# A spectral gated mix on one core: half of the filter loads issued from GpSimd, most exchanges from SyncE, the job list written anew

## The chip, the cores and the metric

The kernel runs on one core of one Trainium2 chip. The metric is the device time of one execution in microseconds. Before the change the median of three runs is 132.87 us (132.73 to 132.93). One more execution was taken with the hardware profiler: 132.51 us, with a span of 130.7 us from its first to its last instruction.

## The reference

```
x = A_x                                   # 1 x 2048 x 1024, bf16
g = sigmoid((x * gate_w).sum(-1, keepdims=True))
a = irfft2(rfft2(x) * (A_w_r + 1j * A_w_i))    # filters 2048 x 513
b = irfft2(rfft2(x) * (B_w_r + 1j * B_w_i))
out = g * a + (1 - g) * b
```

One real image of 2048 rows and 1024 columns is taken to its two-dimensional spectrum, multiplied by two complex filters, taken back twice, and the two results are mixed row by row with a gate. `B_x` is not used.

## The kernel before

The transforms are matrix products on TensorE. The 2048 rows are split as 32 x 64, the columns are folded into four classes of 256. All the work is cut into *jobs*, and one table, `ORDER`, lists the jobs in one order for the whole kernel. A job's name is followed by its arguments; the last letter is the engine or queue that does it (a ScalarE, d VectorE, p GpSimd, s SyncE). `Prog.add` (L202) puts each operation on its engine's list in the order of the table and finds from the keys that it reads and writes which earlier operations it needs; `emit` (L246) then writes each engine's list with waits. So each engine works strictly in its order, and an operation that waits holds up all behind it on that engine, DMA issues included. PSUM is handed out in four units of two banks: a matmul job takes the unit that was given back longest ago (`take`, `give`, L341 to L348), which also follows the table.

The jobs, in the order of the computation:

- `load.x.g.half` brings in one half of group g of x (256 KB, eight groups). `fold` adds and subtracts mirrored columns on VectorE for groups 0 to 3 (`FOLDED`); the others (REV) are only copied in reverse. `s1m`/`s1e`: first row transform (32 points) on TensorE and its eviction from PSUM. `egen` makes signed copies of its matrix E, `sig0` is a first small Sigmoid on ScalarE, `warm` and `keep` are matmuls of zeros.
- `s2m`/`s2e`: the column transform; it needs all of stage 1. `s4m`/`s4e`: the 64-point row transform. Both exist for p = 0 to 7 and for h = 1 and h = 0, the upper and the lower half of the 513 column frequencies.
- `swap.p.h` is an exchange: two DMAs within SBUF that put the even partitions' data on the odd ones and the other way round, 128 KB each. `xneg.p.h` flips signs behind it, on VectorE or ScalarE.
- `load.W.h.b.m.f` loads m blocks of filter f (0 A, 1 B) from block b on, for half h: four DMAs each (real and imaginary part, two row directions), pieces of 512 or 514 bytes. `load.R` loads the odd rows of block 0, two DMAs. Blocks 1, 2 and 3 lie in `WR`, block 0 in `FR`; both halves use the same place, so that a block of the lower half (h = 0) is loaded once the products of the upper half have used the block there. `w5` saves one column of a block.
- `prod.t.h.c.d` multiplies row block t of half h by its filters on VectorE: t = 0 to 3 uses block 0, 4 to 7 block 1, 8 to 15 blocks 2 and 3. With c = 2 all of it, with c = 0 and 1 (t >= 10, lower half) one half each.
- `s5m.g`/`s5e.g`: the inverse 64-point transform. Groups 16 to 31 need all products of the upper half; groups 8 to 15 need those products of the lower half with c = 2 and c = 1; groups 0 to 7 need all of the lower half.
- The gate: `rev`, `gwm`, `gwe`, `gsm`, `gse`, `rowsum`, `stm`, `ste`, `stx`, `stp`, `zsm`, `zse`, `zst`, `zld` make it and spread it over the partitions through DRAM (`zst` writes, `zld` reads); `rb` and `al` multiply it into the matrix U5 of the last row transform.
- `s6m`/`s6e`: inverse 32-point transform with the gate in it. `s7m`, `s7c`, `s7p`: inverse column transform, one eviction on ScalarE and two additions from PSUM on VectorE. `fin` joins mirrored columns, `store` writes the output.

Filter loads before all stand on SyncE, but for the R loads on GpSimd; of the sixteen exchanges seven are on SyncE, seven on GpSimd, two on ScalarE. A DMA issue occupies its queue's engine, and it waits in that queue's order: `dma` is L312/L313, `copy` L315 to L319, `mult` L321/L322, `sign` L324 to L328, `minus` L330 to L334, `mm` L336/L337. The order in `ORDER` comes from a search outside the kernel that works with a table of durations; that table is not in the file.

Of the kernel before, what the change touches and what calls it, by code (L numbers as in the profile page):

```python
# [26 lines left out]
load.W.1.2.2.0.s fold.4.0.d fold.0.0.d s1m.7.0 s1m.7.1 s1m.3.1 s1e.1.1.a s1m.4.1 load.CK.s load.W.1.2.2.1.s fold.0.1.d s1e.7.0.a s1m.0.0
s1e.7.1.a s1e.3.1.a s1m.4.0 s1e.4.1.d s1m.0.1 s1m.3.0 load.R.1.0.1.1.s load.W.1.0.1.0.s s1e.0.0.a s1e.4.0.d s1m.1.0 s1e.0.1.a s1e.1.0.a
s1e.3.0.d load.GR.a keep.5.2 s2m.7.1 s2m.5.1 s2e.7.1.d s2e.5.1.d s2m.4.1 s4m.7.1 s4m.5.1 s2m.0.1 s2e.4.1.d rev s4e.7.1.a swap.7.1.a
s4e.5.1.d swap.5.1.a load.W.1.0.1.1.s s2m.6.1 s4m.4.1 s2e.6.1.d s2m.3.1 s4e.4.1.a s4m.6.1 swap.4.1.s s2e.0.1.d s2e.3.1.a s2m.1.1 s4m.3.1  # L30
xneg.7.1.d prod.14.1.2.d gwm s4e.6.1.a xneg.5.1.d load.W.1.1.1.1.s s2e.1.1.a s4e.3.1.a s4m.0.1 load.R.1.0.1.0.p load.W.1.1.1.0.s
prod.15.1.2.d gwe.a s4e.0.1.a prod.10.1.2.d xneg.4.1.d w5.0.a w5.2.a s2m.6.0 prod.11.1.2.d gsm.12.2 s2e.6.0.a swap.6.1.p gsm.8.2 s4m.1.1
prod.9.1.2.d gse.12.2.a s4e.1.1.a xneg.6.1.d load.VC.s s2m.2.1 swap.1.1.s gsm.10.2 gse.8.2.a prod.8.1.2.d prod.13.1.2.d s2e.2.1.a s4m.6.0
gse.10.2.a gsm.4.2 s4e.6.0.a swap.3.1.p prod.12.1.2.d gse.4.2.a keep.1.2 xneg.1.1.d gsm.6.2 xneg.3.1.a s4m.2.1 prod.6.1.2.d swap.0.1.p
gse.6.2.a prod.3.1.2.d gsm.0.2 w5.1.a s4e.2.1.a xneg.0.1.a swap.6.0.s gse.0.2.a w5.3.a s2m.4.0 s2m.0.0 s2m.5.0 s2e.4.0.a s2e.0.0.a gsm.14.2
gse.14.2.a s4m.4.0 prod.2.1.2.d s2e.5.0.a s4e.4.0.a prod.1.1.2.d s4m.0.0 s4m.5.0 gsm.2.2 s4e.0.0.a gse.2.2.a s2m.2.0 s2m.1.0 swap.2.1.s
prod.0.1.2.d xneg.6.0.d rowsum.0.d s4e.5.0.a prod.7.1.2.d load.W.0.2.2.1.s xneg.2.1.d rowsum.1.d s2e.2.0.a load.W.0.2.2.0.s s2e.1.0.a stm
prod.5.1.2.d swap.4.0.p load.W.0.0.1.0.s s2m.7.0 s2m.3.0 ste.a xneg.4.0.d s4m.1.0 load.W.0.0.1.1.s swap.0.0.p load.R.0.0.1.1.p prod.4.1.2.d
s4m.2.0 s2e.7.0.a s4m.7.0 xneg.0.0.d s2e.3.0.a s4e.1.0.a s4e.2.0.a s4e.7.0.a prod.8.0.2.d stx.s s5m.24 prod.12.0.0.d swap.5.0.p s5m.30
load.R.0.0.1.0.p s4m.3.0 s5e.24.a s5e.30.a rowsum.2.p stp.2.d swap.1.0.s keep.8.2 swap.7.0.s s5m.23 prod.13.0.0.d prod.9.0.2.d stp.0.d  # L40
# [222 lines left out]
def bass_gated_mix__spectral_gfnet__spectral_gfnet__prompt_kernel(nc, A_x, A_w_r, A_w_i, B_x, B_w_r, B_w_i, gate_w, out):  # L263
# [44 lines left out]
    P = Prog()  # L308
# [81 lines left out]

    def keep(k, n):
# [444 lines left out]
```

## Time and profile before

| what | value |
|---|---|
| median of 3 runs | 132.87 us (132.73 to 132.93) |
| the profiled execution | 132.51 us, span 130.7 us |
| TensorE busy | 109.0 us, 83% of the span |
| VectorE busy | 105.1 us, 80% |
| ScalarE busy | 92.5 us, 71% |
| GpSimd busy | 48.8 us, 37% |
| moved by DMA | 25.56 MB, mean 196 GB/s |
| mean granted TensorE clock | 0.961 |

Busy time does not count DMA issues on the hardware queues (SPq, ACTq); those of GpSimd are shown on POOL as instructions of their own. A row in order of time gives start, length, engine, line, operation, tiles and count, and in brackets how long the engine was idle before it and what ended that. In rows of groups the figures behind the bar are busy time, mean duration of one in ns, and idle time before the group.

### The profile page before, as it was taken

The page shows a single profiled execution, that of the slowest core. Times are in us where ns is not written, and L with a number is a line of the kernel's source. Part 1 is how long each engine was busy: PE and PEld are TensorE (multiplying, and loading weights), DVE is VectorE, ACT ScalarE, POOL GpSimd, SP SyncE. Part 2 cuts the span into 40 slices and gives each one's busy share as a digit, 9 for nine tenths or more (in the row PEclk, how much of TensorE's full clock was granted, in tenths as well). Part 3 has the DMA queues.
Part 4 walks back from the last instruction along what each step waited for, and adds up shares of the span by engine and source line. Part 5 has one row for each costly group of instructions (what it writes and reads, how often), then busy time and mean ns, then how long its engine had stood idle before and what let it go on. Part 6 is the DMA issues. An engine that isn't in the chain of part 4 may idle for free.

```text
span 130.7 us, 3713 instructions
## 1 busy us (share of the span) xinstructions
PE 109.0 (83%) x1553; PEld 87.0 (67%) x1553; DVE 105.1 (80%) x135; ACT 92.5 (71%) x121; POOL 48.8 (37%) x58
## 2 busy tenths in 40 slices
PE   6964997899999969979987835999999987999900
PEld 3343876668677756927675525999999986798300
DVE  0216858698999699973999799799979999999990
ACT  0750696521999599998999982999388995679110
POOL 3000000012170002950310000999345894999480
PEclk9997799999999999999999996799999999999995
DMA  3899999978689729999756784600000312174347
GB/s 85 284 351 351 365 327 331 294 167 209 214 222 302 245 90 242 276 346 303 230 183 176 203 271 153 291 0 5 5 0 0 115 50 86 75 278 170 115 151 259
DMA packets 27507, 25.56 MB, mean 196 GB/s; under 512 B 2834, under 2 KB 23074, under 8 KB 27234
## 3 DMA queue, kind: packets, MB, share of 16 engines
q1 hardware_dynamic: 22544, 18.41, 47.4%
q10 hardware_dynamic: 3714, 3.95, 8.9%
q0 software_dynamic: 1232, 2.96, 6.3%
q8 instruction: 12, 0.20, 0.7%
q14 instruction: 5, 0.04, 0.1%
HBM read 16.90 MB, written 4.20 MB: 161 GB/s over the span
## 4 chain that ended last, share of the span: by engine, by line
PE 37%; DMA 20%; DVE 14%; ACT 8%; SPq 7%; issue 6%; ACTq 4%; DVEq 1%
PE PS L337 37%; DMA WP<-in_A_x_dram 9%; DVE WP L322 8%; DMA WR<-in_A_w_i_dram 7%; SPq L313 7%; ACTq L313 4%; ACT WP L317 4%; DVE FR L753 4%; DMA WP<-WP 3%; ACT FR L317 2%; DVE WP L472 1%; ACT L667 1%; ACT WP L332 1%; DVEq L775 1%; DVE WR L753 0%
## 5 line engine op out<-in xcount | busy, mean ns | idle before, releaser
L317 ACT ACTIVATE WP<-PS 128x1024 bf16<-128x1024 f32 (+1 forms) x51 | 49.1, 1019 | 15.2 <-PE PS L337 14.9
L317 ACT ACTIVATE FR<-PS 128x1024 bf16<-128x1024 f32 (+1 forms) x44 | 36.2, 890 | 12.3 <-PE PS L337 9.2
L337 PE MATMUL PS<-FR,WP 128*128 128x128 bf16 (+2 forms) x384 | 32.6, 246 | 1.3 <-DVE FR L753 1.0
L337 PEld LDWEIGHTS PS<-FR,WP 128*128 128x128 bf16 x384 | 28.4, 130 | 5.1 <-DVE FR L753 1.4
L337 PE MATMUL PS<-CK,WP 128*128 128x64 bf16 x512 | 20.2, 202 | 5.4 <-DVE WP L322 4.7
L337 PEld LDWEIGHTS PS<-CK,WP 128*128 128x128 bf16 x512 | 19.3, 119 | 8.0 <-DVE WP L322 5.3
L759 POOL TENSOR_TENSOR WR<-FR 128x512 bf16<-128x512 f32 x15 | 20.4, 1369 | 7.5 <-DVE FR L753 7.2
L319 DVE CAST WP<-PS 128x1024 bf16<-128x1024 f32 x14 | 16.5, 1218 | 3.4 <-PE PS L337 3.3
L753 DVE TENSOR_TENSOR FR<-PS,FR 128x512 f32<-128x512 f32 x28 | 17.7, 678 | 1.2 <-ACT FR L317 1.0
L322 DVE TENSOR_TENSOR WP<-FR,WR 128x1024 bf16<-128x1024 bf16 (+1 forms) x18 | 14.6, 866 | 3.1 <-issue 2.2
L337 PE MATMUL PS<-F,FR 128*128 128x128 bf16 x256 | 15.9, 219 | 1.2 <-ACT FR L317 0.6
L337 PEld LDWEIGHTS PS<-F,FR 128*128 128x128 bf16 x256 | 14.7, 98 | 3.1 <-ACT FR L317 1.6
L337 PE MATMUL PS<-WP 128*128 128x256 bf16 (+1 forms) x128 | 13.4, 265 | 3.8 <-DMA WP<-in_A_x_dram 2.7
L337 PEld LDWEIGHTS PS<-WP 128*128 128x128 bf16 x128 | 10.6, 106 | 6.9 <-DMA WP<-in_A_x_dram 3.5
L322 DVE TENSOR_TENSOR WP<-WP,WR 128x2048 bf16<-128x2048 bf16 x12 | 14.3, 1217 | 0.0
L337 PE MATMUL PS<-FR 128*128 128x480 bf16 (+3 forms) x52 | 11.7, 364 | 2.7 <-ACT WP L317 1.4
L322 POOL TENSOR_TENSOR FR<-FR,F 128x1024 bf16<-128x1024 bf16 x3 | 7.3, 2438 | 16.0 <-DMA FR<-c_U 16.0
L759 DVE TENSOR_TENSOR WR<-FR 128x512 bf16<-128x512 f32 x13 | 12.6, 990 | 0.0
L313 POOL DMA_DIRECT2D FR<-FR x8 | 4.5, 565 | 17.9 <-PE PS L337 17.9
L577 POOL COPY FR<-FR 128x128 bf16<-128x128 bf16 x1 | 0.3, 292 | 27.3 <-DMA FR<-c_RG 27.3
L337 PE MATMUL PS<-WP,CK 128*128 128x512 bf16 (+4 forms) x44 | 8.7, 328 | 0.0
L337 PEld LDWEIGHTS PS<-FR 128*128 128x128 bf16 x52 | 4.2, 112 | 6.5 <-issue 1.6
(54 smaller groups left out, 88.3 us busy)
## 6 DMA issues: line engine op xcount, KB each, us to landing
WP<-in_A_x_dram ACTq DMA_DIRECT2D x9, 256.0 KB, 8.6
out_dram<-WR SPq DMA_DIRECT2D x17, 128.0 KB, 2.1
WP<-in_A_x_dram SPq DMA_DIRECT2D x7, 256.0 KB, 7.9
FR<-FR SPq DMA_DIRECT2D x8, 128.0 KB, 2.9
FR<-FR POOLq DMA_DIRECT2D x8, 128.0 KB, 5.2
FR<-c_U SPq DMA_DIRECT2D x1, 1024.0 KB, 7.2
FR<-c_DI SPq DMA_DIRECT2D x1, 1024.0 KB, 4.8
out_dram<-WR ACTq DMA_DIRECT2D x8, 128.0 KB, 2.3
```

What stands on the lines that cost most here:

```text
L313: return P.add(eng, lambda e: e.dma_start(dst, src), dma=name, **kw)
L317: P.add("act", lambda e: e.activation(dst, src, ACT.Copy), **kw)
L319: P.add(eng, lambda e: e.tensor_copy(dst, src), **kw)
L322: P.add(eng, lambda e: e.tensor_tensor(out=dst, in0=s0, in1=s1, op=ALU.mult), **kw)
L332: P.add("act", lambda e: e.activation(dst, src, ACT.Copy, scale=-1.0), **kw)
L337: P.add("pe", lambda e: e.matmul(o, lh, rh, start=first, stop=last), **kw)
L472: P.add(Q[eng], lambda e: e.tensor_tensor(out=fs, in0=xs(0, 1), in1=xs(511, -1), op=ALU.subtract if k else ALU.add), **kw)
L577: P.add("pool", lambda e: e.tensor_copy(sl(FR, GRo + 128, [(1, 128)]), sl(FR, GRo + 127, [(-1, 128)])), r=["GR"], w=["GRr"])
L667: P.add("act", lambda e: e.activation(sl(ZG, 0, [(1, 32)], np_=64), sl(FR, 20480, [(1, 32)], np_=64), ACT.Sigmoid), r=["zero", ("FR", 40), ...
L753: P.add(Q[eng], lambda e: e.tensor_tensor(out=o, in0=ps(u * 1024, [(1, 512)]), in1=eos(i), op=ALU.subtract if s else ALU.add), r=[("EO", i ...
L759: P.add(Q[eng], lambda e: e.tensor_tensor(out=od, in0=pv[0], in1=pv[1], op=ALU.subtract if s else ALU.add), r=[("PQ", i % NPQ, 0), ("PQ", ...
L775: with nc.Block() as block:
```

## The change

`ORDER` is replaced by another list of the same kinds of jobs. What each job computes is unchanged, and so are `FOLDED`, `HALVED` and `MODE`. In words: x comes in as groups 3, 1, 4, 2, 5, 6, 0, 7 instead of 6, 2, 5, 1, 3, 7, 0, 4; the upper half is transformed from p = 0 upwards and multiplied from block 0 on (t = 1, 0, 3, 2, 4, 6, 5, 7 and then 14 to 12), where it was multiplied from blocks 2 and 3 on; seven of the twelve W jobs stand on GpSimd (28 of 48 DMAs) and five on SyncE; of the exchanges nine are on SyncE, six on GpSimd, one on ScalarE. The gate vector's load (`load.GR`) stands on ScalarE right behind x instead of behind stage 1. `egen.1.2` comes ahead of `sig0`. Of `rb` and `al`, two of four `rb` more are on VectorE. `warm` and `sig0` get one more key to wait for, because block 0 is now also written from GpSimd's queue. The new file is one line shorter ahead of the code, so that a line's number there is one less than here.

The start of the table, and the other edits:

```diff
-load.SM.a zero load.E.1.s load.x.6.0.a warm.12x64x1.14x512x1 load.x.6.1.s load.x.2.1.a egen.1.3 egen.1.1 fold.6.0.d load.x.5.1.s
+load.SM.a zero load.E.1.s egen.1.3 load.x.3.0.a load.E.0.s load.x.3.1.a egen.0.1 fold.3.0.d fold.3.1.d load.x.1.0.a egen.1.1 load.x.1.1.a
...
-                    mm(ps(u * 1024, [(1, nn)]), sl(FR, 20480, [(st, 128)]), sl(FR, 20480, [(1, nn)]), True, True, r=["zero", ("FR", 40), ("FR", 41)], w=banks(u))
+                    mm(ps(u * 1024, [(1, nn)]), sl(FR, 20480, [(st, 128)]), sl(FR, 20480, [(1, nn)]), True, True, r=["zero", ("FR", 40), ("FR", 41), ("W", 3, 1)], w=banks(u))
...
-        P.add("act", lambda e: e.activation(sl(ZG, 0, [(1, 32)], np_=64), sl(FR, 20480, [(1, 32)], np_=64), ACT.Sigmoid), r=["zero", ("FR", 40), ("FR", 41)], w=["ZG"])
+        P.add("act", lambda e: e.activation(sl(ZG, 0, [(1, 32)], np_=64), sl(FR, 20480, [(1, 32)], np_=64), ACT.Sigmoid), r=["zero", ("FR", 40), ("FR", 41), ("W", 3, 1)], w=["ZG"])
```

What stands on GpSimd from `rev` on, before (WP<-WP and FR<-FR are exchanges of the upper and the lower half, FR<-in_ are filter rows of block 0):

```order
L577 COPY FR<-FR 128x128 [waits d_GR]
L313 DMA FR<-in_A_w_r_dram 64x257
L313 DMA FR<-in_A_w_i_dram 64x257
L313 DMA WP<-WP 64x1024 [waits s_act]
L313 DMA WP<-WP 64x1024
```

And in the new order (64x4x257 is 256 pieces of 514 bytes; WR<-in_ are blocks 2 and 3 here):

```order
L576 COPY FR<-FR 128x128 [waits d_GR]
L312 DMA FR<-in_A_w_r_dram 64x257
L312 DMA FR<-in_A_w_i_dram 64x257
L312 DMA FR<-in_B_w_r_dram 64x4x257 [waits s_act,s_pe]
L312 DMA FR<-in_B_w_i_dram 64x4x257
L312 DMA FR<-in_B_w_r_dram 64x3x257
L312 DMA FR<-in_B_w_i_dram 64x3x257
L312 DMA FR<-in_A_w_r_dram 64x4x257
L312 DMA FR<-in_A_w_i_dram 64x4x257
L312 DMA FR<-in_A_w_r_dram 64x3x257
L312 DMA FR<-in_A_w_i_dram 64x3x257
L312 DMA WR<-in_A_w_r_dram 64x8x257
```

Eight loads of block 0 and, from the last of these rows on, eight of blocks 2 and 3 with 512 pieces each (`load.W.1.2.2.0` and `.1`) now stand on GpSimd ahead of its first exchange.

On SyncE, behind the loads of x and of the constants, before (from the fourth exchange on):

```order
L313 DMA WP<-WP 64x1024 [waits s_act]
L313 DMA WP<-WP 64x1024
L313 DMA WR<-in_B_w_r_dram 64x8x256 [waits d_W121,s_act,s_dve]
L313 DMA WR<-in_B_w_i_dram 64x8x256
L313 DMA WR<-in_B_w_r_dram 64x8x256
L313 DMA WR<-in_B_w_i_dram 64x8x256
L313 DMA WR<-in_A_w_r_dram 64x8x256 [waits d_W120]
L313 DMA WR<-in_A_w_i_dram 64x8x256
```

And in the new order, at the same place in the computation:

```order
L312 DMA FR<-FR 64x1024 [waits s_pe,s_act]
L312 DMA FR<-FR 64x1024
L312 DMA WR<-in_A_w_r_dram 64x8x256 [waits d_W120,s_dve]
L312 DMA WR<-in_A_w_i_dram 64x8x256
L312 DMA WR<-in_A_w_r_dram 64x8x256
L312 DMA WR<-in_A_w_i_dram 64x8x256
L312 DMA FR<-FR 64x1024 [waits s_pe,s_act]
L312 DMA FR<-FR 64x1024
```

SyncE issues only filter A of the lower half's blocks 2 and 3 (`load.W.0.2.2.0`), and does so behind four exchanges of the lower half; filter B's four loads (`load.W.0.2.2.1`) stand on GpSimd behind `rowsum.2` and `swap.4.0`.

On VectorE, the sign flips (TENSOR_SCALAR) and the first products of the upper half, before (the d_xs semaphores are exchanges, d_W filter loads):

```order
L328 TENSOR_SCALAR WP<-WP,SM 128x1024 [waits s_act,d_xs71]
L322 TENSOR_TENSOR WP<-WP,WR 128x8x64x4 [waits d_W121,d_W120,s_dve]
L328 TENSOR_SCALAR WP<-WP,SM 128x1024 [waits d_xs51]
L322 TENSOR_TENSOR WP<-WP,WR 128x8x64x4
L322 TENSOR_TENSOR WP<-WP,WR 128x8x64x4 [waits s_dve]
```

And in the new order:

```order
L327 TENSOR_SCALAR WP<-WP,SM 128x1024 [waits s_act,d_xs01]
L321 TENSOR_TENSOR WP<-WP,FR 128x8x64x4 [waits d_R100,d_W101,d_R101,d_W100,s_dve]
L321 TENSOR_TENSOR WP<-WP,FR 128x8x64x4
L318 CAST GSB<-PS 128x4 [waits s_pe]
L321 TENSOR_TENSOR WP<-WP,FR 128x8x64x4 [waits d_xs11,s_act]
L321 TENSOR_TENSOR WP<-WP,FR 128x8x64x4
L327 TENSOR_SCALAR WP<-WP,SM 128x1024 [waits d_xs21]
L327 TENSOR_SCALAR WP<-WP,SM 128x1024 [waits d_xs31]
L321 TENSOR_TENSOR WP<-WP,WR 128x8x64x4 [waits d_W111,d_W110,s_dve]
```

The first product now waits for block 0, which GpSimd loads; blocks 2 and 3, also GpSimd's, are wanted by the ninth product.

More of the change, by code (lines that the diff above doesn't have):

```diff
@@ L27 @@
[L27 to L38, printed above, removed]
```

63 lines of the change are left out of this document (37 added, 26 removed).

## Prediction

> **What bounds the kernel now.** I read the chain of waits first, then the stretches of time with each engine's busy time, then the order of time on VectorE (DVE), ScalarE (ACT), GpSimd (POOL) and SyncE (SP). From the chain, in order of time (start, length, what):
>
> ```profile
> 7.28 12.18 DMA WP<-in_A_x_dram
> ...
> 41.77 4.26 DMA WP<-WP
> ...
> 52.31 7.16 DMA WR<-in_A_w_i_dram
> 59.47 2.16 issue
> ...
> 71.23 2.34 DMA WR<-in_A_w_i_dram
> ...
> 79.88 10.38 PE PS L337 x272
> ```
>
> Up to 19.46 us (7.28 + 12.18) the image x is loading. Then one exchange (WP<-WP) and two filter loads (WR<-in_A) stand on the chain, and at 79.88 the products are done and TensorE can transform them. The stretches (start:end, length, then busy us and count of PE, weight load, DVE, ACT, POOL, then clock, DMA share, GB/s):
>
> ```profile
> 33.40:59.10 25.70, 23.45 (x350) 17.40 (x348) 23.02 (x28) 24.09 (x39) 9.13 (x17) 1.00 0.80 242
> 59.10:79.80 20.70, 15.03 (x281) 11.23 (x281) 17.61 (x25) 18.37 (x22) 1.71 (x3) 1.00 0.77 226
> ...
> 91.30:127.50 36.20, 31.44 (x368) 27.31 (x368) 34.68 (x49) 23.77 (x34) 26.04 (x24) 1.00 0.26 95
> ```
>
> From 33.4 to 79.8 DVE (products) and ACT (PSUM evictions) are both close to full: ACT lacks 1.6 us in the first stretch, DVE 2.7; in the second 2.3 and 3.1. So exchanges and filter loads cost only what DVE or ACT waits for them, and what one wins counts only as far as the other follows. After 91.3 DVE sets the pace (34.68 of 36.20). DVE's waits, in brackets:
>
> ```profile
> 33.42 0.48 DVE L328 TENSOR_SCALAR WP<-WP,SM 128x1024 bf16<-128x1024 bf16 x1
> ...
> 46.06 0.49 DVE L328 TENSOR_SCALAR WP<-WP,SM 128x1024 bf16<-128x1024 bf16 x1 [1.46 <-DMA WP<-WP]
> ```
> ```profile
> 57.44 0.49 DVE L328 TENSOR_SCALAR FR<-FR,SM 128x1024 bf16<-128x1024 bf16 x1 [0.97 <-DMA FR<-FR]
> 57.84 1.22 DVE L322 TENSOR_TENSOR WP<-WP,WR 128x2048 bf16<-128x2048 bf16 x1
> ...
> 61.63 1.83 DVE L322 TENSOR_TENSOR WP<-FR,WR 128x2048 bf16<-128x2048 bf16 x2 [2.17 <-issue]
> ...
> 74.59 8.24 DVE L322 TENSOR_TENSOR WP<-FR,WR 128x2048 bf16<-128x2048 bf16 x10 [0.91 <-DVE PST L322]
> ```
>
> The upper half (h=1) is multiplied from 33.42 to 59.06, the lower half to 82.83. Late transfers cost 1.46 + 0.97 in the one, 2.17 + 0.91 in the other ("issue" ends with load.W.0.2.2.0, the chain's 7.16 us row). Why those loads come late stands on SP's queue:
>
> ```profile
> 47.51 0.65 SPq L313 DMA_DIRECT2D WR<-in_B_w_r_dram  x1
> ...
> 52.31 1.15 SPq L313 DMA_DIRECT2D WR<-in_A_w_i_dram  x1
> ...
> 59.79 0.61 SPq L313 DMA_DIRECT2D FR<-in_B_w_i_dram  x1
> ```
>
> From 47.51 to 60.40 SP does nothing but issue sixteen filter loads, one after another, and every exchange given to it waits behind them.
>
> **The change, part by part.** The sum is made against the profiled execution, 132.51 us (span 130.7); the median of the three runs, 132.87, lies 0.36 above, which I add at the end.
>
> *Loading x and stage 1.* The same bytes in another order, so the last piece of x still lands at about 19.5. Group 7 (a REV group) is now folded behind group 0 on DVE, so some 0.5 us more stand between that landing and the first s2 matmul. ACT now meets a Copy before the Sigmoid, so two tables are loaded instead of one:
>
> ```profile
> L667 ACT ACT_TABLE_LOAD x1 | 1.3, 1283 | 3.6 <-issue 3.6
> ```
>
> That is 1.28 us more, near 7 to 11 us, before x gives ACT much to do; counted at 0 while x hides it, 1.3 if it does not.
>
> *The first exchange.* Now it is swap.0.1, behind three evictions on ACT (s2e.0.1, s2e.1.1, s4e.0.1); before, one stood in front of it:
>
> ```profile
> 28.50 1.02 ACT L317 ACTIVATE WP<-PS 128x1024 bf16<-128x1024 f32 x1 [3.81 <-PE PS L337]
> 29.55 2.59 ACTq L313 DMA_DIRECT2D WP<-WP  x4
> ```
>
> ACT starts at about 26.35 (28.50 less the DVE evictions that led it, plus the 0.5) and issues the exchange at about 30, 0.5 later than 29.55; the sign flip then starts at about 34.0 instead of 33.42. Bounds: 0 to 1.5 us late.
>
> *GpSimd's loads, the price the trace lacks.* POOL now waits for the gate vector (issued on ACT right behind x, so about 20 to 21 instead of 28.8), then issues two R loads, eight loads of block 0 (192 or 256 pieces each) and eight of W.1.2.2 (512 pieces), all before its first exchange. The nearest rows are 64 pieces (the x4 rows and the first) and 128 (the last):
>
> ```profile
> L577 POOL COPY FR<-FR 128x128 bf16<-128x128 bf16 x1 | 0.3, 292 | 27.3 <-DMA FR<-c_RG 27.3
> ```
> ```profile
> 29.06 0.69 POOL L313 DMA_DIRECT2D FR<-in_A_w_r_dram  x1
> ...
> 37.18 2.16 POOL L313 DMA_DIRECT2D WP<-WP  x4 [0.66 <-ACT GW L317]
> 51.46 2.34 POOL L313 DMA_DIRECT2D FR<-FR  x4 [12.13 <-PE PS L337]
> ...
> 65.17 0.63 POOL L313 DMA_DIRECT2D zd<-ZG  x1 [1.04 <-ACT ZG L663]
> ```
>
> 64 pieces take 0.54 (2.16 / 4), 128 take 0.63: 1.4 ns for each further piece, so a 512-piece load takes 0.54 + 448 x 0.0014 = 1.17. Bounds: 0.54 (no cost per piece; the first of a row of issues takes 0.69 anyway), and 4.3 (all of 0.54 proportional: 8.4 ns a piece). I take 1.17, since the 128-piece row is nearest. Then POOL has issued the R loads by 22.5, block 0 by 28.6 (8 x 0.76) and W.1.2.2 by 38.0 (8 x 1.17). Landing, by queue and size:
>
> ```profile
> WR<-in_A_w_r_dram SPq DMA_DIRECT2D x2, 257.0 KB, 11.6
> FR<-FR SPq DMA_DIRECT2D x8, 128.0 KB, 2.9
> FR<-FR POOLq DMA_DIRECT2D x8, 128.0 KB, 5.2
> ```
>
> With 3 to 6 us more, block 0 is there at 32 to 34 (needed at 34.4) and W.1.2.2 at 41 to 44 (needed by the ninth product, about 46.8). Both lie beside the stage-2 work; the margins are about 1 and 3 us.
>
> *Upper half on DVE.* Durations:
>
> ```profile
> L322 DVE TENSOR_TENSOR WP<-WP,WR 128x2048 bf16<-128x2048 bf16 x12 | 14.3, 1217 | 0.0
> L322 DVE TENSOR_TENSOR WP<-FR,WR 128x1024 bf16<-128x1024 bf16 x12 | 7.8, 687 | 0.0
> L328 DVE TENSOR_SCALAR WP<-WP,SM 128x1024 bf16<-128x1024 bf16 x9 | 4.2, 481 | 5.3 <-DMA SM<-c_SM 3.6 <-DMA WP<-WP 1.7
> L319 DVE CAST WP<-PS 128x1024 bf16<-128x1024 f32 x14 | 16.5, 1218 | 3.4 <-PE PS L337 3.3
> ```
>
> Back to back these overlap by 0.08: 1.14 a product, 0.61 a half product, 0.40 a flip, 1.14 an eviction. From its first flip the new order holds 16 products (18.2), six flips (2.4), a small cast and a row-sum step (0.8): 21.4. SP now has nothing but exchanges then, so the waits fall from 2.4 to my estimate of 1.5 (xneg.1.1 on ACT and xneg.3.1, whose exchanges go out just ahead of their use; bounds 0.5 to 4). The upper half ends at 34.0 + 21.4 + 1.5 = 56.9, 2.2 earlier than 59.06.
>
> *Lower half on DVE.* Up to where s5 group 8 may start: ten products (11.4), six half products (3.7), five flips (2.0), the second row-sum step, one s5 eviction and a trifle (1.9): 19.0, so 75.9; six more halves (3.7) end at 79.6, against 82.83. Blocks 0 and 1 are freed and reloaded some 12 us before use. W.0.2.2.0 and W.0.2.2.1 are freed last, at 56.9; SP issues its four by 59.5, POOL, behind rowsum.2 and swap.4.0, by about 63.8 (59.1 + 4 x 1.17). They land by 67; the first half product wants them at 68: no wait, where 2.17 + 0.91 stood. Bounds 0 to 3.
>
> *ACT.* Rows:
>
> ```profile
> L317 ACT ACTIVATE WP<-PS 128x1024 bf16<-128x1024 f32 x50 | 48.7, 1030 | 15.2 <-PE PS L337 14.9
> L326 ACT ACTIVATE FR<-FR,SM 128x1024 bf16<-128x1024 bf16 x2 | 2.3, 1156 | 0.0
> ```
> ```profile
> 59.90 1.94 ACT L317 ACTIVATE WP<-PS 128x1024 bf16<-128x1024 f32 x2 [0.34 <-PE PS L337]
> ...
> 71.35 6.49 ACT L317 ACTIVATE WP<-PS 128x1024 bf16<-128x1024 f32 x7
> 80.96 10.35 ACT L317 ACTIVATE WP<-PS 128x1024 bf16<-128x1024 f32 x11 [3.12 <-PE PS L337]
> ```
>
> An eviction costs 0.93 in a row (6.49 / 7), a flip 1.05. ACT starts 2.15 earlier, takes three more upper-half evictions (2.8) and one more flip, and issues one exchange less (1.3): at about 60 it stands where it stood at 59.55. Then come 15 s5 evictions and one s4 (14.8), two flips (2.1) and the gate (0.2), to 77.1, about when group 8 is ready (75.9 + 0.7 of matmul). The 3.12 us wait at 80.96 goes; the rest of s5 is the same row, 10.35, plus 0.9 for the groups that wait for DVE's last halves: 88.3, against 80.96 + 10.35 = 91.31. DVE meanwhile has five evictions (5.7) and the small work of the gate, and is done by about 88 too. **Gain 3.0 us.** U5 and the gate are on time if they come as early as before; they wait for POOL's zst, now behind swap.7.0, so up to 1 us may go here.
>
> *The tail* keeps the 32 PSUM additions and 13 final additions on DVE (34.68 busy of 36.20): 0, give or take 1. Sum: 132.51 - 3.0 = 129.5, on the median's scale 129.9; I say **129.8**, 127.3 to 131.3 by the bounds above except POOL's.
>
> **The rivals.**
>
> *POOL's long loads are dearer (slower).* With p for a 512-piece load, W.1.2.2 has landed at 22.5 + 8 x (0.54 + 0.4 (p - 0.54)) + 8p + 4 = 29.1 + 11.2p. It delays the ninth product from p = 1.58, costs 1.12 us per 0.1 us beyond it, and eats the gain at p = 1.85. At p = 2.0 it is +4.7: 134.5; at 4.3 far more. For it: no row has over 128 pieces. Against: 64 to 128 pieces cost only 0.09. Chance 0.17.
>
> *VectorE holds up GpSimd's issues (slower).* The products fill DVE almost without a break while POOL issues W.0.1.1.1, W.0.1.1.0 and W.0.2.2.1. If each issue waited out a product, the four of W.0.2.2.1 would come 4 x 1.2 = 4.9 later, at 72 instead of 67: 4 us of wait, 133.5 or so. The x4 row at 51.46 speaks against it: POOL issued four exchanges in 2.34 us with DVE multiplying throughout. Chance 0.07. The Trainium skill (SBUF — State Buffer, § SBUF: two separate sides) says that while VectorE runs in a two-port mode GpSimd cannot write the descriptors of its DMAs, and that SP or ACT should issue them instead, which speaks against this change; by that row the trace does not agree.
>
> *ACT is the bound anyway (about the same).* It was short of work by only 1.6 us of 25.70. If the new order makes it wait 2.5 us for the exchanges whose flips it does in its own queue (1.1, 5.1, 5.0, 4.0, 7.0), where the old had two or three, the gain shrinks to 0.5: 132.4, spread 131.4 to 133.3. Chance 0.20.
>
> **How the numbers follow.** The forecast has 0.56. The measurement tells 0.2% (0.27 us). Faster: 0.56 + 0.10 of the ACT rival = 0.66; same: 0.08 of it; slower: 0.02 of it + 0.17 + 0.07 = 0.26. The range reaches from 127.3 up to 134.5, which takes in the ACT and VectorE rivals and the near end of the first.
>
> **What would show it.** Right: POOL issues of 512 pieces near 1.2 us, W.1.2.2 issued by 40; no DVE wait over 1 us between 45 and 57; the last half product before 81; ACT without the 3 us gap; the first PSUM addition of s7 3 us earlier. Wrong: POOL issues over 1.6 us or DVE waiting for W.1.2.2; ACT idle behind its flips; rb waiting for U5; or new waits in the tail.

## The result and the profile after

The changed kernel took 140.1 us (median of 4 runs, 137.81 to 141.3) beside 132.8 for the kernel before. Two of the four (141.3 and 141.01 us) were slow runs with a lower granted TensorE clock (0.922 and 0.945, beside 0.963 and 0.951 in the others), and the ratio, 1.043 with a 95% interval of 1.034 to 1.052, leaves them out, as all ratios below do with such runs. It is slower, and outside the range of the prediction. In the first profile of it stage 1 is late (128 products in 14.0 us instead of 11.9) and all that follows is shifted, so the comparison is made with a second profile of the same kernel (run `e8_same` below: 139.21 us, span 137.3). Both have the same waits. The group of stage 1's products, first profile and second:

```profile
L336 PE MATMUL PS<-WP 128*128 128x256 bf16 (+1 forms) x128 | 14.0, 278 | 3.6 <-DVE WP L471 3.6
```
```profile
L336 PE MATMUL PS<-WP 128*128 128x256 bf16 (+1 forms) x128 | 11.9, 246 | 3.6 <-DVE WP L471 2.4 <-DVE WP L318 1.0 <-DMA WP<-in_A_x_dram 0.2
```

Where the steps of the prediction came out (us; read from the order of time on VectorE, ScalarE and the queues; a transfer lands at its issue plus its time to landing; "last half product" is the end of the lower half's products):

| | before | forecast | after |
|---|---|---|---|
| first exchange, issued to landed | 29.55 to 33.29 | 30 to 34 | 30.26 to 37.12 |
| first sign flip | 33.42 | 34.0 | 37.14 |
| upper half multiplied | 59.06 | 56.9 | 59.01 |
| last half product | 82.83 | 79.6 | 85.05 |
| stage 5 ends | 91.31 | 88.3 | 94.65 |
| first addition of stage 7 | 95.61 | | 98.74 |
| VectorE ends | 127.45 | | 133.01 |
| span | 130.7 | | 137.3 |

The chain of waits of the changed kernel (second profile), the first exchange and the filter load that stand on it:

```profile
30.26 0.53 ACTq L312
30.83 6.29 DMA WP<-WP
37.14 0.50 DVE WP L327
...
65.26 8.54 DMA WR<-in_B_w_i_dram
```

Before, a later exchange stood on the chain with 4.26 us, and two filter loads with 7.16 and 2.34; now the first exchange has 6.29 and one load 8.54. VectorE's order of time, waits in brackets (second profile):

```profile
37.14 0.49 DVE L327 TENSOR_SCALAR WP<-WP,SM 128x1024 bf16<-128x1024 bf16 x1 [4.71 <-DMA WP<-WP]
...
52.24 1.23 DVE L321 TENSOR_TENSOR WP<-WP,WR 128x2048 bf16<-128x2048 bf16 x1 [0.25 <-ACT WP L325]
...
73.92 0.69 DVE L321 TENSOR_TENSOR WP<-FR,WR 128x1024 bf16<-128x1024 bf16 x1 [1.87 <-DMA WR<-in_B_w_i_dram]
```

One wait of 4.71 us ahead of the first flip, then almost none to the end of the upper half: the new order does hold VectorE's work together, as forecast, but starts it 3.1 late. ScalarE, whose flip waits for an exchange too, stands behind it:

```profile
38.92 1.15 ACT L325 ACTIVATE WP<-WP,SM 128x1024 bf16<-128x1024 bf16 x1 [3.21 <-issue]
```

What GpSimd does meanwhile (first and last load of block 0, first and last of the two 1 MB loads of blocks 2 and 3):

```profile
24.76 0.62 POOL L312 DMA_DIRECT2D FR<-in_B_w_r_dram  x1
...
27.86 0.64 POOL L312 DMA_DIRECT2D FR<-in_A_w_i_dram  x1
28.49 0.71 POOL L312 DMA_DIRECT2D WR<-in_A_w_r_dram  x1
...
33.26 0.69 POOL L312 DMA_DIRECT2D WR<-in_B_w_i_dram  x1
```

A 512-piece load costs 0.69, so the 2 MB are all issued by 33.9, four us earlier than forecast, and lie on the DMA engines just when the exchanges are issued. The final additions on VectorE, in the kernel before and in the changed one:

```profile
L759 DVE TENSOR_TENSOR WR<-FR 128x512 bf16<-128x512 f32 x13 | 12.6, 990 | 0.0
```
```profile
L758 DVE TENSOR_TENSOR WR<-FR 128x512 bf16<-128x512 f32 x13 | 15.4, 1214 | 0.0
```

Thirteen in both, but 2.8 us more on the engine that sets the tail. The mean hides two sizes: in the kernel before three of the thirteen took 1.8 to 2.2 us and the others 0.67 to 0.81, in the changed one five took 1.7 to 2.4 and the others 0.68 to 0.87.

### The profile page after: what moved, and what is told of

It reads as the page before. It is cut to its first block, busy times and chain, and to the rows that moved or that the text cites. A ratio compares the mean times of both kernels' runs of the same rounds, so it can differ in the third digit from the quotient of the medians.

```text
span 139.4 us, 3701 instructions
## 1 busy us (share of the span) xinstructions
PE 112.7 (81%) x1553; PEld 89.4 (64%) x1553; DVE 106.9 (77%) x136; ACT 98.1 (70%) x125; POOL 61.1 (44%) x79
## 4 chain that ended last, share of the span: by engine, by line
PE 47%; DVE 17%; ACT 12%; DMA 11%; issue 6%; ACTq 2%; DVEq 1%
PE PS L336 47%; ACT WP L316 9%; DMA WP<-in_A_x_dram 6%; DVE WP L321 5%; DMA WP<-WP 5%; DVE WR L758 5%; DVE FR L752 5%; ACTq L312 2%; ACT FR L316 2%; ACT FR L325 1%; DVEq L774 1%; DVE FR L318 1%; DVE WP L471 1%; DVE WR L752 0%; DVE WP L327 0%
## 5 line engine op out<-in xcount | busy, mean ns | idle before, releaser
L316 ACT ACTIVATE WP<-PS 128x1024 bf16<-128x1024 f32 (+1 forms) x55 | 53.1, 1030 | 12.3 <-PE PS L336 11.9
L336 PEld LDWEIGHTS PS<-CK,WP 128*128 128x128 bf16 x512 | 20.2, 120 | 6.5 <-ACT WP L316 2.3
L336 PE MATMUL PS<-CK,WP 128*128 128x64 bf16 x512 | 21.3, 206 | 3.1 <-ACT WP L316 1.5
L336 PE MATMUL PS<-F,FR 128*128 128x128 bf16 x256 | 16.6, 223 | 5.0 <-DVE GSB L318 3.9
L318 DVE CAST WP<-PS 128x1024 bf16<-128x1024 f32 x10 | 12.1, 1222 | 5.3 <-PE PS L336 5.3
L321 DVE TENSOR_TENSOR WP<-FR,WR 128x1024 bf16<-128x1024 bf16 (+1 forms) x18 | 14.4, 865 | 2.1 <-DMA WR<-in_A_w_i_dram 2.1
L336 PEld LDWEIGHTS PS<-WP 128*128 128x128 bf16 x128 | 11.6, 111 | 6.3 <-DVE WP L471 4.6
L758 DVE TENSOR_TENSOR WR<-FR 128x512 bf16<-128x512 f32 x13 | 15.4, 1212 | 0.0
L336 PE MATMUL PS<-FR 128*128 128x480 bf16 (+3 forms) x52 | 11.9, 375 | 3.1 <-ACT WP L316 1.7
L327 DVE TENSOR_SCALAR WP<-WP,SM 128x1024 bf16<-128x1024 bf16 x9 | 4.2, 483 | 9.1 <-DMA WP<-WP 5.5
L336 PE MATMUL PS<-WP,CK 128*128 128x512 bf16 (+4 forms) x44 | 9.6, 358 | 0.0
L471 DVE TENSOR_TENSOR WP<-WP 128x1024 bf16<-128x1024 bf16 x8 | 5.2, 685 | 5.3 <-DMA WP<-in_A_x_dram 5.3
```

The costliest lines, as they stand in the source:

```text
L316: P.add("act", lambda e: e.activation(dst, src, ACT.Copy), **kw)
L318: P.add(eng, lambda e: e.tensor_copy(dst, src), **kw)
L321: P.add(eng, lambda e: e.tensor_tensor(out=dst, in0=s0, in1=s1, op=ALU.mult), **kw)
L327: P.add(eng, lambda e: e.tensor_scalar(out=dst, in0=src, scalar1=SM[:, col:col + 1], scalar2=None, op0=ALU.mult), **kw)
L336: P.add("pe", lambda e: e.matmul(o, lh, rh, start=first, stop=last), **kw)
L471: P.add(Q[eng], lambda e: e.tensor_tensor(out=fs, in0=xs(0, 1), in1=xs(511, -1), op=ALU.subtract if k else ALU.add), **kw)
```

## The experiments

Theory A: the filters' bytes that are issued ahead of an exchange, from whichever queue, have to cross the DMA engines first; the new order puts a 1 MB load there. Rival B: stage 1 and the tail lose the time. Rival C: GpSimd's queue pushes the exchanges aside. Theory D: the new tail is dearer by itself. Rival E: ScalarE's row sets the half's end whatever VectorE waits for.

### The 2 MB later

```diff
-gse.6.2.d load.W.1.2.2.0.p swap.2.1.s
+gse.6.2.d swap.2.1.s
...
-swap.7.1.p swap.4.1.p
+swap.7.1.p load.W.1.2.2.0.p swap.4.1.p load.W.1.2.2.1.p
```

> The changed kernel, with the two 1 MB filter loads of the upper half's blocks 2 and 3 put later on GpSimd, one behind each of its first two exchanges, so that they are issued after about 37 us instead of 28.4 to 33.8. Theory A (these 2 MB share the DMA engines with the first exchanges): the first exchange, issued near 31.4 us, lands within 4 us instead of 7.1, the first half product starts by 36 instead of 39.0, the idle times of VectorE (5.5), ScalarE (3.4) and TensorE (3.9 us) go, and the time falls by 2 to 6 us to 134 to 138; the 9th product may now wait for the load, which would eat a part. Rival B (the late stage 1, the tail and the slower final additions make up most of the loss): the exchange may land earlier, but the time falls by less than 1.5 us.

Measured: 144.7 us, 1.091 (1.083 to 1.100). VectorE's order of time:

```profile
32.35 0.49 DVE L327 TENSOR_SCALAR WP<-WP,SM 128x1024 bf16<-128x1024 bf16 x1 [0.54 <-DMA WP<-WP]
...
53.37 4.63 DVE L321 TENSOR_TENSOR WP<-WP,WR 128x2048 bf16<-128x2048 bf16 x4 [4.97 <-DMA WR<-in_B_w_i_dram]
```

The mechanism is as A says: the exchange took 2.7 us and the first flip came 4.8 earlier. The time, 12 us above the kernel before, is a miss for A as for B: the loads, issued from 39.6 and 43.4 on, landed at 46.7 and 53.2, and the 9th product, due at 44.4, waited for an exchange (3.54) and then for them.

### All filter loads from SyncE

```diff
-load.VC.s load.W.1.0.1.0.p
+load.VC.s load.W.1.0.1.0.s load.W.1.2.2.0.s load.W.1.2.2.1.s
...
-load.W.0.1.1.1.p
+load.W.0.1.1.1.s
```

and so on for each `load.W` and `load.R` of GpSimd's; the two 1 MB loads are gone from their later places.

> The changed kernel with all its filter loads issued from SyncE's queue again, in the changed kernel's order, the two 1 MB loads still ahead of the first exchanges and issued at about the same time, 28 to 35 us. Theory A (bytes on the engines at the wrong time, whichever queue issues them): the first exchange lands as late as before, after 37.5 us, and the time stays within 2 us of the changed kernel's 140. Rival C (GpSimd's software queue, with its larger packets, takes the engines' time from the exchanges' small packets): the exchange that ScalarE issues lands within 4 us, by 35.5, and the time falls by over 2 us.

Measured: 147.8 us, 1.115 (1.106 to 1.124). The flip:

```profile
35.28 0.49 DVE L327 TENSOR_SCALAR WP<-WP,SM 128x1024 bf16<-128x1024 bf16 x1 [3.29 <-DMA WP<-WP]
```

The exchange took 5.4 us, between the two expectations: it landed at 35.26, before C's 35.5, but took more than C's 4 us, with three of the first 1 MB load's four transfers ahead of its second DMA. The time is a miss for both. SyncE's own exchanges went out only at 35.4, behind the loads, and the second landed at 40.6. So GpSimd's queue is not the only cause, and without it the order is worse.

### The kernel before with one part of the change

```diff
-load.W.1.1.1.1.s
...
-load.R.1.0.1.0.p load.W.1.1.1.0.s
+load.R.1.0.1.0.p load.W.1.1.1.1.p load.W.1.1.1.0.p
```

(The two loads stood ahead of and behind other jobs; only they moved. They are the two of block 1, not of blocks 2 and 3 as the expectation has it.)

> The kernel before, with one part of the change alone: the two 0.5 MB loads of blocks 2 and 3 counted from the low end (issued by SyncE at 34.5 to 39.9 us before) are issued from GpSimd at 30.3 to 35.3 us, beside the first exchange (issued at 29.55, landed 3.7 us later) and the second (30.9, landed 4.5 us later). Theory A: those two exchanges land 1 to 3 us later, and the first half product starts 1 to 3 us after 33.9; the loads themselves land earlier, so the time is 0 to 2 us longer. Rival C gives the same direction but more: over 3 us on the exchanges, as the software packets go first. Rival B: no change in either, within 0.5 us.

Measured: 133.1 us, 1.003 (0.998 to 1.008): no change that can be told. The flip:

```profile
35.65 0.49 DVE L328 TENSOR_SCALAR WP<-WP,SM 128x1024 bf16<-128x1024 bf16 x1 [1.96 <-DMA WP<-WP]
```

The exchange took 5.9 us instead of 3.7 and the next 6.3 instead of 4.5, but the loads, earlier now, spared as much later: the upper half ended at 58.83 (59.06 before). In that order, then, a later first exchange cost nothing in the end: the wait of 1.46 at 46.06 went.

### The 2 MB held until the first exchange has landed

```diff
             kw = dict(w=keys) if what == "W" else dict(w=[("WR16", f)])
+            if (h, b) == (1, 2):
+                kw["r"] = place(2, 0, 1)[2]
```

> The changed kernel, with the two 1 MB filter loads of the upper half's blocks 2 and 3 made to wait on GpSimd until the first exchange has landed (about 32.5 us), between the changed kernel's 27.3 to 33.8 and the 39.6 to 46.2 of the run that put them behind GpSimd's exchanges. Theory A (2 MB have to cross the DMA engines between the first exchange and the 9th product; the start decides who waits): the first product starts near 33, the loads land near 43 to 44.5, the 9th product (due at 44 to 45 then) waits 0 to 1 us, the last upper product ends near 56 instead of 59.1, and the time falls by 2 to 4 us against the changed kernel's 138 to 140. Rival B (what is lost lies in the lower half and the tail, which start by TensorE and ScalarE, not by this): the upper half ends earlier and the time falls by less than 1 us.

Measured: 137.9 us, 1.041 (1.035 to 1.048), 0.8 below the changed kernel of its group.

```profile
33.49 0.49 DVE L327 TENSOR_SCALAR WP<-WP,SM 128x1024 bf16<-128x1024 bf16 x1 [0.55 <-DMA WP<-WP]
40.90 0.49 DVE L327 TENSOR_SCALAR WP<-WP,SM 128x1024 bf16<-128x1024 bf16 x1 [1.25 <-DMA WP<-WP]
44.29 0.49 DVE L327 TENSOR_SCALAR WP<-WP,SM 128x1024 bf16<-128x1024 bf16 x1 [2.91 <-DMA WP<-WP]
```

The first exchange came in 2.7 us; the third and fourth, now behind the loads, took 6.5 and 8.0. Most of the wait moved behind the fourth product, and the upper half ended at 60.20, not near 56: A holds for each exchange, but the gain that was expected of it does not. B's figure (less than 1 us) came, but not its reason, as the upper half ended no earlier.

### One load early from SyncE; then both

```diff
-load.R.1.0.1.1.s
+load.R.1.0.1.1.s load.W.1.2.2.0.s
...
-gse.6.2.d load.W.1.2.2.0.p swap.2.1.s
+gse.6.2.d swap.2.1.s
```

> The changed kernel with one of the two 1 MB loads of blocks 2 and 3 (upper half, first filter) issued from SyncE at 21 us, behind its R load, where SyncE's queue ran dry and the DMA engines were 70% busy, instead of from GpSimd at 27 to 28.5. Theory A (the bytes that are still to come when the first exchanges go out decide): about 0.7 MB more is over by 28 us, the first exchange lands 1.5 to 3 us earlier than 37.1, the time falls by 0.5 to 2 us against 138.7; block 0's filters may land 1 to 3 us later than 30.5, still ahead of the first product. Rival C (it is GpSimd's queue that pushes the exchanges aside): as one of the two still comes from GpSimd, the first exchange gains less than 1 us.

Measured: 138.2 us, 1.041 (1.030 to 1.052). The bytes were over by 36.8 instead of 41.6, the exchange landed at 37.27 all the same. That misses A's 1.5 to 3 us and is what C expected. The run that followed moves `load.W.1.2.2.1` there as well:

> The run with one 1 MB load issued early from SyncE, with the other one behind it on SyncE too, so that GpSimd's queue holds block 0's filters alone and nothing of it is on the way when the first exchange goes out (29.7 us). Rival C (GpSimd's queue pushes the exchanges aside): the exchange lands within 4.5 us, by 34.3, and the time falls by 1.5 to 3 us against 138.2. Theory A (the bytes, whichever queue): the exchange lands with the last of the filters again, at 36 to 37.5, and the time stays within 1 us.

Measured: 137.6 us, 1.030 (1.019 to 1.040). The first flip in these two:

```profile
37.30 0.49 DVE L327 TENSOR_SCALAR WP<-WP,SM 128x1024 bf16<-128x1024 bf16 x1 [5.39 <-DMA WP<-WP]
```
```profile
36.35 0.49 DVE L327 TENSOR_SCALAR WP<-WP,SM 128x1024 bf16<-128x1024 bf16 x1 [4.60 <-DMA WP<-WP]
```

In the second run GpSimd's queue held block 0 alone. The last of that landed at 33.38, yet the exchange took 6.7 us (7.5 with 1 MB of GpSimd's beside it) and landed at 36.33, with SyncE's load: C falls as the main cause. Set side by side, the exchange lands within 0.7 us of the last filter transfer that was issued ahead of its second DMA, or, where that was over before, 2.1 us after that DMA's issue. What is issued behind it (the changed kernel's second 1 MB, landed at 41.62) does not hold it:

| run | first exchange issued | transfers ahead of it all landed by | it landed | took |
|---|---|---|---|---|
| 2 MB later | 29.64 | 30.52 | 32.32 | 2.7 |
| before | 29.55 | 33.96 | 33.29 | 3.7 |
| all on SyncE | 29.83 | 35.41 | 35.26 | 5.4 |
| both early, SyncE | 29.59 | 36.16 | 36.33 | 6.7 |
| changed kernel | 30.26 | 36.62 | 37.12 | 6.9 |
| one early | 29.75 | 36.78 | 37.27 | 7.5 |

The Trainium skill (DMA: Bandwidth & Descriptors, § Issuing engines are not separate DMA queues) says that DMAs started by any engine run on the same 16 DMA engines and interleave; the 6.7 against 7.5 agrees.

### The lower half: loads sooner; loads left out

```diff
-rowsum.2.p
+load.W.0.2.2.0.p load.W.0.2.2.1.p rowsum.2.p
...
-load.W.0.2.2.0.s prod.2.0.2.d
+prod.2.0.2.d
...
-swap.6.0.s prod.6.0.2.d swap.4.0.p
+swap.4.0.s swap.6.0.s prod.6.0.2.d
```

> The changed kernel with both loads of the lower half's blocks 2 and 3 issued from GpSimd as soon as the last upper product frees their place (59.1 us), where one was queued on SyncE behind three exchanges (61.1) and one on GpSimd behind an exchange (63.3); that exchange goes to SyncE. Theory A for the lower half (2 MB that can't start before the upper half has ended keep VectorE waiting 1.9 us, and hold up the exchanges of panels 6 and 7, as in the upper half): the loads land 2 to 4 us earlier, near 70 to 71, the wait before the first product of blocks 2 and 3 goes, and the time falls by 1 to 2 us. Rival (stage 5's evictions on ScalarE set the end of the half): the wait goes and the time falls by less than 0.5 us.

Measured: 139.3 us, 1.045 (1.038 to 1.051). The wait for the filters went, and another came:

```profile
67.77 0.48 DVE L327 TENSOR_SCALAR FR<-FR,SM 128x1024 bf16<-128x1024 bf16 x1 [1.89 <-DMA FR<-FR]
```

From the last upper product to the last landing it took 14.4 us, 14.8 in the changed kernel, so A's landing 2 to 4 us earlier failed: issuing sooner brought hardly any bytes sooner. The time did not fall, as the rival had it, but because the wait moved and not because of ScalarE. Then without them:

```diff
+            if (h, b) == (0, 2):
+                return
             kw = dict(w=keys) if what == "W" else dict(w=[("WR16", f)])
```

> The changed kernel without the two loads of the lower half's blocks 2 and 3 (2 MB; its products use the upper half's filters, which lie in the same place). If these bytes hold up the lower half: the exchanges of panels 6, 4 and 7 and the statistics' two small ones, which took 4.4 to 9.5 us, take under 3.5, the 1.9 us wait goes, the last half product ends 2 to 3 us earlier than 85.05 and the time falls by 1.5 to 3 us. If ScalarE's row of evictions sets the half's end: the waits go, and the time falls by less than 0.7.

Measured: 134.9 us, 1.017 (1.006 to 1.028). The exchange of panel 6 took 2.6 us instead of 9.4, no wait for a transfer is left in the lower half, the last half product ended at 82.09 (85.05), stage 5 at 90.98 (94.65). The row of products with which the lower half ends, in the changed kernel and without the loads:

```profile
74.93 10.12 DVE L321 TENSOR_TENSOR WP<-FR,WR 128x2048 bf16<-128x2048 bf16 x14
```
```profile
71.97 10.12 DVE L321 TENSOR_TENSOR WP<-FR,WR 128x2048 bf16<-128x2048 bf16 x14
```

These 2 MB cost about 3 us (2.3 in the lower half, 0.7 in stage 5); E falls. No queue can start them before the upper half has ended, because the new order uses blocks 2 and 3 last there; the kernel before uses them first, and its loads of the same blocks went out from 47.51.

### The tail

Three runs: the changed kernel with the tail of before, the kernel before with the changed tail (in both all `rb`, `al`, `s6`, `s7`, `fin` and `store` jobs in the other's order, behind the rest), and the last store alone on SyncE:

```diff
-store.12.1.a store.15.0.p
+store.12.1.a store.15.0.s
```

> The changed kernel up to the end of stage 5, then stages 6, 7, the final additions and the stores in the order and on the engines of the kernel before. From the first product of stage 7 to VectorE's end the kernel before took 31.8 us and the changed one 34.2 to 34.3. Theory D (the tail's order costs 2.4 us of the loss by itself, because VectorE's final additions run beside GpSimd's: 1,212 ns each instead of 990): the time falls by 2 to 3 us against the changed kernel's 138 to 140. Rival (the tail is late only because what feeds it is late): less than 0.7 us.

> The converse of the run with the tail of the kernel before: the kernel before up to the end of stage 5, then stages 6, 7, the final additions and the stores in the order and on the engines of the changed kernel. Theory D (the tail's order costs about 2.4 us by itself, and GpSimd's closing drain behind its late store about 1): the stretch from the first product of stage 7 to VectorE's end grows from 31.8 to about 34.3 and the time by 2.4 to 3.5 us, to 134.8 to 136. Rival: by less than 0.7.

> The changed kernel with its last store on GpSimd (tile 15, first half) issued from SyncE. GpSimd's closing drain took 5.0 us behind that store and ended the span 1.3 us after SyncE was done. If the drain sets the end, the time falls by about 1.3 us, to 138.7; if SyncE's waits for the stores set it anyway, by less than 0.4 us.

Measured, in this order: 136.6 us beside the changed kernel's 138.7 (no interval; the runs lay between 133.95 and 138.22); 138.5, 1.041 (1.029 to 1.053); 138.3, 1.044 (1.036 to 1.052). The stretch from the first addition of stage 7 to VectorE's end, by engines, for the changed kernel with the tail of before and for the kernel before with the changed one:

```profile
100.23:132.03 31.80, 27.13 (x309) 23.17 (x308) 31.40 (x45) 22.11 (x31) 24.08 (x22) 1.00 0.29 107
```
```profile
99.39:133.69 34.30, 26.92 (x308) 22.79 (x306) 34.19 (x45) 20.94 (x29) 25.09 (x23) 1.00 0.28 104
```

The 2.5 us between these go with the tail, not with what stands ahead of it: D holds. The time of the second run is a miss: the kernel before lost more than D's 2.4 to 3.5, 6.2 at VectorE's end, because three `rb` steps came to stand behind stage 5 on VectorE in this edit (2.1 more from stage 5's end to stage 7) and stage 5 ended 1.6 later; so only the stretch tells. The store's 0.4 is within the runs' spread; behind VectorE's last instruction the span went on for 3.5 us with it on SyncE, 4.3 with it on GpSimd.

All 28 final additions on VectorE (the first two of the fifteen that change):

```diff
-fin.0.1.p s7m.3 al.2.1.a s7c.2.a fin.0.0.p
+fin.0.1.d s7m.3 al.2.1.a s7c.2.a fin.0.0.d
```

> The changed kernel with all 28 final additions on VectorE and none on GpSimd. Theory D (VectorE's and GpSimd's final additions shut each other out, which makes VectorE's 1,212 ns instead of about 690): each takes 0.68 to 0.72 us, VectorE's tail grows by only 15 x 0.61 - 13 x 0.52 = 2.4 us, and the time is 140 to 142. Rival (1,212 ns is what such an addition costs on VectorE in this place): the tail grows by over 15 us.

Measured: 141.4 us (no interval; the runs lay between 138.49 and 142.32), and

```profile
L758 DVE TENSOR_TENSOR WR<-FR 128x512 bf16<-128x512 f32 x28 | 18.2, 682 | 0.0
```

With none on GpSimd such an addition takes 0.68 every time; what lies above that in the mean of 1.21 is waiting for GpSimd's additions: each of the five long ones of the changed kernel ran beside one of GpSimd's for 0.6 to 1.3 us. VectorE's tail grew by 1.9 us for fifteen more. The Trainium skill (SBUF — State Buffer, § SBUF: two separate sides) calls the port that the two share an exclusive lock, held for a whole instruction, for operations of this kind; the 682 against 1,214 ns agrees.

### Queues alone; the kernel before with loads timed

Four loads of block 1 to GpSimd and six of GpSimd's seven exchanges to SyncE, by their last letters alone, the list in the order of before:

```diff
-load.W.1.1.1.1.s
+load.W.1.1.1.1.p
...
-swap.6.1.p
+swap.6.1.s
```

> The kernel before with queues changed alone, its job list left in its order: four of its eight pairs' later filter loads (block 1 of both halves) from GpSimd, and its six exchanges of GpSimd's from SyncE. Theory A (the order of the jobs, which puts 2 MB ahead of the first exchanges and a dearer tail, is what costs; the queues in themselves cost little): within 1.5 us of 132.4. Rival C: 135 or more.

Measured: 135.4 us, 1.020 (1.010 to 1.029), more than A allowed and within C's 135 or more. But C's reason is not what the trace shows: SyncE has loads of before's order in front of its new exchanges, and this one went out at 54.30, where GpSimd's had gone out at 51.46:

```profile
61.35 0.48 DVE L328 TENSOR_SCALAR FR<-FR,SM 128x1024 bf16<-128x1024 bf16 x1 [4.03 <-DMA FR<-FR]
```

And three loads on GpSimd at times picked from the trace of before (the first is also made to wait for the first exchange):

```diff
-load.R.1.0.1.0.p
+load.R.1.0.1.0.p load.W.1.1.1.1.p
...
-load.W.0.2.2.1.s
+load.W.0.2.2.1.p
...
-rowsum.2.p
+rowsum.2.p load.W.0.1.1.0.p
```

> The kernel before, with three of its filter loads moved to GpSimd, each at a time that its exchanges leave free: block 1's first filter of the upper half waits for the first exchange's landing (33.3 us), one of the lower half's blocks 2 and 3 goes out when its place is free (47.5, beside SyncE's), and one of the lower half's block 1 at 59.1 instead of 66.1 to 69.3. Theory A (GpSimd's queue is no harm in itself; what counts is which bytes are ahead of which exchange): the waits of the kernel before at 46.06 (1.46), 61.63 (2.17) and 74.59 (0.91) shrink or go, and the time falls by 1 to 4 us to 128.5 to 131.5. Rival C (the software queue's packets hurt any exchange beside them): exchanges beside those loads take over 6 us, and the time is the same or longer. Rival E (ScalarE's row sets the half's end anyway): the waits go and the time stays within 0.7 us.

Measured: 134.7 us, 1.018 (1.007 to 1.028). A and E missed. C's figures came: the time is longer, and three exchanges beside the first of these loads took 6.9 us each. C's reason did not: GpSimd's four transfers had all landed by 40.93, and the three exchanges landed at 43.71 to 45.79, as did the last of SyncE's load and its constant ahead of them (44.33 and 45.61).

```profile
43.73 0.48 DVE L328 TENSOR_SCALAR WP<-WP,SM 128x1024 bf16<-128x1024 bf16 x1 [2.78 <-DMA WP<-WP]
...
67.22 0.19 DVE L322 TENSOR_TENSOR PST<-XST,W 128x64 bf16<-128x64 bf16 x1 [1.59 <-DMA XST<-XST]
```

The waits at 46.06, 61.63 and 74.59 shrank or went, others came: 6.0 us from the first flip on instead of 5.7. The kernel before from 50 to 60 us (columns as in the prediction; the DMA share is the last but one):

```profile
50.00:60.00 10.00, 8.89 (x130) 6.53 (x128) 8.49 (x11) 9.66 (x14) 5.80 (x11) 1.00 1.02 303
```

The DMA engines have nothing to spare there; a load sooner was an exchange later.

### The changed kernel again, and repaired

> The changed kernel as it is, once more beside the others of this group: 137.8 to 141.3 us as in its first runs, with a profile in which stage 1's 128 products take 12.1 us as in the run with the store moved, not 14.0, so that first exchange, upper end, lower end and tail can be set against the kernel before.

Measured: 138.7 us, 1.045 (1.036 to 1.054). Its profile is the one read above. Then both loads early, with the tail of before:

> Both loads early from SyncE, as in the run beside it, and the tail of the kernel before. If the two repairs add up (2.1 to 3 us for the tail, 0.5 to 3 for the loads): 133 to 135.5, at best level with the kernel before. If what the one wins the other would have hidden: 136 to 137.

Measured: 134.9 us, 1.010 (1.002 to 1.018), 2.7 below the run with the loads alone: the repairs add up. Last, on top of these two, the second 1 MB behind three exchanges, and a ready product into the wait:

```diff
-load.W.1.2.2.0.s load.W.1.2.2.1.s
+load.W.1.2.2.0.s
...
-swap.3.1.s
+swap.3.1.s load.W.1.2.2.1.s
```
```diff
-prod.7.0.2.d keep.8.2 prod.10.0.1.d
+prod.7.0.2.d keep.8.2 prod.4.0.2.d prod.10.0.1.d
```

> The run with both loads early and the tail of the kernel before, but with the second 1 MB load issued by SyncE behind its third exchange (about 37 us) instead of at 24 to 29. Theory A (an exchange lands when the filters issued ahead of it have landed): 1 MB less is ahead of the first exchange, which lands at 32.5 to 34 instead of 36.5; the load lands at 43 to 46, about when the 9th product wants it (44); the upper half ends 1.5 to 3 us earlier than 57.9, and the time falls by 1 to 3 us from 133.6, to 130.5 to 132.5. If the wait only moves to the 9th product: within 0.7 us of it.

> As the run beside it, with one product of the lower half that is ready (tile 4) moved ahead of the first one that waits for the last 2 MB of filters, so that 1.14 us of work fill a wait of 2.0. If VectorE's half products set when stage 5's second group of eight may start: 0.7 to 1.2 us faster than the run beside it. If ScalarE's row does: the same within 0.3.

Measured: 131.6 us, 0.988 (0.983 to 0.993), and 130.5 us, 0.982 (0.975 to 0.988): both a little faster than the kernel before, with intervals clear of 1. VectorE in the last one:

```profile
32.34 0.49 DVE L327 TENSOR_SCALAR WP<-WP,SM 128x1024 bf16<-128x1024 bf16 x1 [0.89 <-DMA WP<-WP]
...
44.80 0.49 DVE L327 TENSOR_SCALAR WP<-WP,SM 128x1024 bf16<-128x1024 bf16 x1 [0.34 <-DMA WP<-WP]
...
68.60 0.69 DVE L321 TENSOR_TENSOR WP<-FR,WR 128x1024 bf16<-128x1024 bf16 x1 [0.70 <-DMA WR<-in_A_w_i_dram]
```

The first exchange took 4.1 and 3.0 us, the held load landed at 45.0 and 44.3, about 1 us ahead of the 9th product, and the upper half ended at 56.4 and 55.4. That is the prediction's 56.9, reached once the exchange is on time. The ready product cut the wait ahead of the first half product from 1.74 to 0.70.

## Why the prediction was wrong

*The step that failed* is the term for the first exchange, and its reason stands in the part on GpSimd's loads: "Both lie beside the stage-2 work; the margins are about 1 and 3 us." I asked when the loads would land and who wanted them, not what they lie in front of. The loads were in fact early, and the first exchange, which I gave 0.5 us of delay with bounds of 0 to 1.5, was 3.1 later than forecast: it took 6.9 us and not 4, and 2.7 in the run that put the loads behind it. The same slip stands under "SP now has nothing but exchanges then": I counted the waits by the queue that issues an exchange, where the runs show that all queues share what lies ahead. The rows were there: in the median a transfer of an exchange within FR took 5.2 us from GpSimd, whose row at 51.46 stands beside SyncE's sixteen loads, and 2.9 from SyncE.

The profiled 139.21 against the forecast 129.5, by stretches:

- *Upper half* ends 2.1 late: 3.1 of the exchange, less 1.2 of waits that I had allowed for later ones (1.5 forecast, 0.25 came), and 0.2 in the work.
- *Lower half*: 26.0 us instead of 22.7, 3.3 late. "They land by 67" failed: 71.95 and 73.80, 14.8 us after their place was free, where I had given 10; the exchange of panel 6 among them took 9.4. The run without these loads has 23.7: 2.3 of the 3.3. The 1.0 that is left is about a wait of 1.09 for TensorE's first stage-5 group, which that run has as well.
- *Stage 5*: 9.6 instead of 8.7, 0.9 late, of which 0.7 goes with the loads. To the first addition of stage 7 4.1 instead of 4.3, 0.2 early.
- *The tail*: "0, give or take 1" was 2.4; I counted the operations on VectorE and not which of them meet GpSimd's. Behind VectorE's end 1.0 more, of which 0.8 goes with the last store on GpSimd.

Together 2.1 + 3.3 + 0.9 - 0.2 + 2.4 + 1.0 = 9.5, to 139.0. About 5 of it (2.1, 2.3 and 0.7) is transfers that wait for filters or filters that are waited for, 3.4 the tail and the end. Rival B of the experiments thus holds for the tail, not for stage 1.

*What was right*: the 21.4 us of work in the upper half (37.14 to 59.01 is 21.9 with 0.25 of waits); and stage 1, 0.3 late by the exchange's issue at 30.26.

*The rivals.* Dear loads on GpSimd: false, 0.69 us for 512 pieces against a threshold of 1.58 (and against the 1.17 that the sum took, so the line through 64 and 128 pieces was too steep); the kernel came out slower by another way. VectorE holding up the issues: false, as these rows of the second profile show, three products without a break and a load issued beside them (the prediction's row at 51.46 is four transfers, so two exchanges and not four):

```profile
48.50 3.49 DVE L321 TENSOR_TENSOR WP<-WP,WR 128x2048 bf16<-128x2048 bf16 x3
```
```profile
48.83 0.66 POOL L312 DMA_DIRECT2D WR<-in_B_w_r_dram  x1
```

What the Trainium skill says of such issues (SBUF — State Buffer, § SBUF: two separate sides) is said of VectorE's two-port modes; no run here shows that these products run in one, so neither this row nor the prediction's speaks against it. ScalarE the bound: it did wait for its flip (3.21), but as a consequence, and with the exchanges on time and the tail of before the kernel came out 1.2 and 1.8% faster, where 2.3% had been forecast. No rival priced the first exchange itself late, though an exchange stood on the chain of waits.

Open: how the DMA engines share their time between the queues. The exchange took 5.4 us beside SyncE's loads alone and 6.9 beside GpSimd's, but three transfers of 257 KB were ahead of its second DMA in the one and four in the other, which fits the bytes. With the same bytes ahead it took 6.7 when both 1 MB loads came from SyncE and 7.5 when one came from GpSimd; whether these 0.8 us are the queue's or come from the issue times is not shown.

## What to carry to other kernels

A small transfer on the chain of waits has to be costed with all bytes issued ahead of it, on every queue; hold bulk loads that are wanted later until it is out, but only so long that they still land on time. An order that uses a block of filters last also brings its next load last. Where the DMA engines are full, another queue or an earlier issue moves a wait and does not remove it: look for work that is ready to fill it, or for an order that needs the bytes later. Additions with both inputs in SBUF on VectorE and GpSimd are to be ordered so that they don't meet.

## What the hardware showed that I had not expected

A filter load issued from GpSimd costs nearly the same whatever its pieces: 0.62 to 0.67 us with 192 or 256, about 0.70 with 512. An exchange of two 128 KB transfers took 2.5 to 2.7 us on free DMA engines and up to 9.4 among 2 MB of filters. A final addition on VectorE takes 682 ns alone and 1,214 on the mean of thirteen when GpSimd's run beside some of them, single ones two us and more.
